# A second fold in a backward row DFT, and its loads spread over the stage before

## The chip, the cores and the metric

The kernel runs on one core of a Trainium2 chip. The metric is the device time of one launch in microseconds; where several runs are shown, it is their median. A core has a matrix engine (TensorE, PE in the profile, with its weight loads shown apart as PEld), three elementwise engines (VectorE or DVE, ScalarE or ACT, GpSimd or POOL), and a queue from which all of this kernel's transfers are issued (SyncE or SP). Matrix products land in PSUM and are copied out by ScalarE or VectorE, which is called an evacuation here.

## The reference

The program computes a two-part block and all of its gradients. With x of 2048 x 448 values in bf16:

- part A: `h = x + irfft2(rfft2(layernorm(x)) * (w_r + 1j*w_i))`, a two-dimensional Fourier filter over rows (448) and columns (2048);
- part B: `out = h + mlp(layernorm(layernorm(h)))`, where the MLP mixes along the 2048 axis: `u = gelu(h^T w1 + b1)`, `y = u w2 + b2`, with 1792 hidden units;
- then the gradients of x, w_r, w_i, w1, b1, w2 and b2 for a given gradient of the output.

The backward pass runs through the MLP first. Its last product gives the gradient of h, called dh. The Fourier filter's backward pass then takes a row DFT of dh, a column DFT, a multiplication with the conjugate filter, and the inverse of both. A DFT is done here as matrix products with tables of cosines and sines. A row of 448 real values has 225 frequencies, kept as 226 columns.

## The kernel before, in words

The 2048 rows are 16 tiles of 128. One Python function writes the whole program; the order of TensorE, VectorE, ScalarE and SP instructions is that of the code. Only GpSimd's instructions are placed by a scheduler. A helper `evac` sends each evacuation to ScalarE or VectorE by a running account of both loads. `defer` puts a transfer some time later in the order of issue.

**The dh stage** is the loop `for t in range(NT)` near line 1183. For tile t, 14 matmuls of 448 columns multiply a transposed tile of w1 (`wT`, four of them in a ring, loaded by a transposing DMA `load_w1T` four tiles ahead) with `du`, the gradient at the hidden layer. The product is normalized back: `ln_a` (one ScalarE operation that leaves PSUM, one small GpSimd operation and one VectorE reduction) and `ln_b` (three VectorE operations), which leaves the tile in `dh`.

**The row DFT** follows inside the same loop, three tiles behind (`LAG`). A row of 448 values is folded first, since cosines are even and sines odd about the middle: `fold_prep`, once for two tiles, writes the sum and the difference of the row's first half and its reversed second half (two VectorE operations of 448 elements). The fold lies in a ring `fold_ring`, three places in the backward pass. `row_a` then takes four pieces of a tile's fold as weights, with a permuting DFT over short groups of rows as the moving side: four matmuls of 128 columns. Its evacuated result is the weights of `row_b`, which does the DFT along the row: for cosine and sine each (index w), two matmuls of 226 columns are summed in PSUM, one for each half of the folded 224 values (index b). Their contraction is 112 deep. The table is `csF`, with a place for each w and b. After every second `row_b`, a transfer regroups the result into `D2`, which the column DFT reads. The regrouping is called the reshuffle here.

**After the loop**, the last rows are done (`for t in range(NT - LAG, NT + 2)`), with matmuls of a weight gradient between them. These come from a list `pending` of generators, from which `fill(n)` takes n steps; they feed on pieces transposed by DMA (`st_load`, of the GELU output in `rE` first) and write weight gradients to memory from `rO` and `rG`. Before the column DFT starts, 40 steps are taken. The column DFT and the filter are in `s2_stage`.

**The loads around it.** The filter W, stored in memory as `w_d` in the forward pass, is read back into `rC` by one load of 1.8 MB after the loop; `rC` holds the output gradient tiles (`go_pt`) until then, the last of which is read by `ln_b` of tile 15. The second weight gradient needs `du` transposed: `load_du`, four transposing transfers of 14 blocks of 128 x 128, issued in `s2_stage` after column groups 3, 7, 11 and 15, into the space of `D2` as that becomes free.

`m448` is a ring of eight 448-element buffers in `r448`; `ln_a` takes two of them for a tile.

Of the kernel before, what the change touches and what calls it, by code (L numbers as in the profile page):

```python
# [13 lines left out]
ALU = mybir.AluOpType  # L14
# [3 lines left out]
P = 128  # L18
S = 2048
D = 448  # L20
DF = 225
KW = 226
F = 1792
NFB = 14
NT = 16
NG = 16
KC = 113
DC = 112
# [11 lines left out]
N_FILL_B = (16, 16, 40, 8, 24, 8)  # L40
INV_SD = 1.0 / float(S * D)
# [78 lines left out]
def kernel(  # L120
# [20 lines left out]
    nc = tc.nc  # L141
# [3 lines left out]
    ve = Meter(nc.vector, load, 1)  # L145
# [68 lines left out]
    def mm(out, lhsT, rhs, start, stop):  # L214
        nc.tensor.matmul(out, lhsT=lhsT, rhs=rhs, start=start, stop=stop)  # L215
        clock[0] += int(np.prod(rhs.shape[1:])) / 2400.0
        run_due()
# [19 lines left out]
    r448 = region("r448", 8 * D)  # L237
# [5 lines left out]
    csF = mem.tile([P, 2, 2, KW], BF16, name="csF")  # L243
# [38 lines left out]
    w_d = dram.tile([P, NG * 2 * KW], BF16, name="w_d")  # L282
# [346 lines left out]
    def fold_prep(src, t2):  # L629
        ft = fold_ring.next()  # L630
        s0 = 2 * t2
        fv = ft[:, 0:2 * D].rearrange("p (s w j) -> p s w j", s=2, w=2)
        a = src[:, s0:s0 + 2, 0:D // 2]
        r = src[:, s0:s0 + 2, D - 1:D // 2 - 1:-1]
        ve.tensor_tensor(out=fv[:, :, 0, :], in0=a, in1=r, op=ALU.add)
        ve.tensor_tensor(out=fv[:, :, 1, :], in0=a, in1=r, op=ALU.subtract)
        folds[t2] = ft

    def row_a(t, R):
        pa = ps_ff()  # L640
        ft = folds[t // 2]
        for k in range(4):
            o = DC * (4 * (t % 2) + k)
            mm(pa[:, k * P:(k + 1) * P], lhsT=ft[:, o:o + P], rhs=R, start=True, stop=True)
        if t % 2 == 0:
            blks[t // 2] = blk_ring.next()
        evac(out=blks[t // 2][:, :, t % 2, :], in_=pa[:].rearrange("p (a b) -> p a b", a=8))

    def row_b(h):
        u, c = divmod(h, 2)  # L650
        if u < 0 or u >= NT // 2:
            return
        pd = ps_ff()
        pv = pd[:, 0:452].rearrange("p (c k) -> p c k", c=2)
        for w in (1, 0):
            for b in range(2):
                mm(pv[:, 1 - w, :], lhsT=blks[u][0:DC, 2 * (2 * w + b) + c].rearrange('p j x -> p (j x)'), rhs=csF[0:DC, w, b, :],
                   start=(b == 0), stop=(b == 1))
        if c == 0:
            css[u] = cs_ring.next()  # L660
        cs = css[u]
        evac(out=cs[:, c], in_=pv)
        if c:
            defer(RESH_LAG, lambda: nc.sync.dma_start(out=D2[u:u + 121:8].rearrange("p g c k -> p (g c k)"),
                                                      in_=cs.rearrange("p x c k -> p (x c k)")), cs)

    def s2_stage(get_x, on_mult, ml, n_fill, gap, make_inv, after_fwd=None, scale=None):
        flush()
        nh = NG // 2
        xs, ys = {}, {}  # L670

        lag = 2 + ml
        for c2 in range(nh + lag):
            if c2 < nh:
                xs[c2] = get_x(c2)
                if make_inv and c2 < 4:
                    gen_inv_s(4 + c2)
                    if c2 in (1, 2):
                        gen_inv_d(c2 - 1)
            for i in range(2):  # L680
                if make_inv and c2 >= 3:
                    next(wp, None)
                    next(wp, None)
                if c2 < nh:
                    g = 2 * c2 + i
                    px = ps_ff()
                    pv = px[:, 0:452].rearrange("p (c k) -> p c k", c=2)
                    mm(pv, lhsT=Vt[:, g, :], rhs=D2[:, g, :, :], start=True, stop=False)
                    mm(pv[:, 0, :], lhsT=Ut[:, g, :], rhs=D2[:, g, 1, :], start=False, stop=False)
                    mm(pv[:, 1, :], lhsT=Un[g], rhs=D2[:, g, 0, :], start=False, stop=True)  # L690
                    evac(out=xs[c2][:, i, :, :], in_=pv, scale=scale)
                if c2 >= lag:
                    s2_inv(2 * (c2 - lag) + i, ys[c2 - lag][:, i, :, :])
                if after_fwd is not None and c2 < nh and g % 4 == 3:
                    after_fwd(g // 4)
                fill(n_fill)
            if ml <= c2 < nh + ml:
                ys[c2 - ml] = on_mult(c2 - ml, xs[c2 - ml])
        if make_inv:
            sc.activation(out=warm, in_=eps_h, func=ACT.Sqrt)  # L700
        fill(gap)
# [56 lines left out]
    pending = []  # L758
# [105 lines left out]
    for c in range(2):  # L864
        sc.copy(out=Rp.rearrange("p (a q b c) -> p c a q b", c=2, q=8, a=4)[:, c],
                in_=Rm[:, 64 * c:64 * c + 64].rearrange("p (q a b) -> p a q b", q=8, a=4))
# [259 lines left out]
                         op0=ALU.mult)  # L1126
    gp_.memset(csF[:, 0, :, 0:1], 0.5)
    ve.tensor_scalar(out=csF[:, :, :, 224:225], in0=csF[:, :, :, 224:225], scalar1=0.5, scalar2=None, op0=ALU.mult)


    dh = cut(rA, 0, NT, D)
    lcol = mem.tile([P, 2 * NT, 3], F32, name="lcol")
# [21 lines left out]
        gen_neg(cut(r2, (2 * NG * KW + 8 * i * P), 8, P), Ut[:, 8 * i:8 * i + 8, :])  # L1154
    Un[:] = [r2[:, 2 * NG * KW + g * P:2 * NG * KW + (g + 1) * P] for g in range(NG)]
    LAG = 3
    st_ring = Ring(ring(rst, 0, 2, 7, P).views + [cut(rS, 6336, 7, P)])
    fold_ring.views.pop()
    order = [(rE, j) for j in range(NFB // 2)] + [(rB, t) for t in range(NT // 2)]
# [2 lines left out]
    def st_load():  # L1162
        if order:
            reg, j = order.pop(0)
            st = st_ring.next()
            nc.sync.dma_start_transpose(out=st, in_=reg[:, j * 1024 + 64:j * 1024 + 960])
            ahead.append(st)


    def rows(t):  # L1170
        if t < NT:
            row_a(t, Rm[:])
        fill(2)
        row_b(t - 2)
        fill(2)

    for t in range(NT):
        wT = w1Ts.pop(0)
        pdh = ps_mm()
        for j in range(NFB):  # L1180
            mm(pdh[:, 0:D], lhsT=wT[:, j, :], rhs=du[:, j, :], start=(j == 0), stop=(j == NFB - 1))
        if t + 4 < NT:
            load_w1T(t + 4)
        pb, tmp, m1, m2, _ = ln_a(t, pdh[:, 0:D], rstd_h[:, t:t + 1], hln[:, t, :], (1.0 + LN_EPS) / D)
        ln_b(pb, tmp, m1, m2, hln[:, t, :], go_pt[:, t, :], dh[:, t, :])
        if t % 2:
            fold_prep(dh, t // 2)
        if t >= NT - 2:
            st_load()
        if t >= LAG:  # L1190
            rows(t - LAG)


    du_t = cut(r2, 0, NFB, 4, P)

    def load_du(q):
        nc.sync.dma_start_transpose(out=du_t.rearrange("p j b q -> p (j b) q")[:, 14 * q:14 * q + 14, :],
                                    in_=rD[:, 14 * P * q:14 * P * (q + 1)])
    def bwd_x(c2):
        return X_ring.next()  # L1200

# [14 lines left out]
    def gw_gen(n, rhs, width, store, ost):  # L1216
        for u in range(n // 2):
# [19 lines left out]
            for c in range(0, 4, 2):  # L1237
# [20 lines left out]

    pending.append(gw_gen(NFB, lambda c, k, a, b: goT[a:b, k, c * 512:(c + 1) * 512], S,
                          lambda j, a, n, o: nc.sync.dma_start(out=out_6[j * P:(j + 1) * P, a:a + n], in_=o[:, 0:n]), ost))  # L1260
    pending.append(gw_gen(NT, lambda c, k, a, b: du_t[a:b, 4 * c:min(NFB, 4 * c + 4), k, :], F,
                          lambda t, a, n, o: nc.sync.dma_start(out=o4[:, t, a:a + n], in_=o[:, 0:n]),
                          Ring(ring(rG, 0, 8, S // 2).views + ost.views)))
    nc.sync.dma_start(out=rC[:, 0:NG * 2 * KW], in_=w_d[:])
    for t in range(NT - LAG, NT + 2):
        if t == NT - 2:
            fill(8)
# [2 lines left out]
        gen_neg(UTn[:, 8 * i:8 * i + 8, :], UTt[:, 8 * i:8 * i + 8, :])  # L1270
    fill(N_FILL_B[2])
    Meter.slack = 4.0
    s2_stage(bwd_x, bwd_mult, 0, N_FILL_B[3], N_FILL_B[4], False, load_du, 2.0 * INV_SD)
    Meter.slack = 2.0
    g_out = w_io(W_view_B, out_2, out_3, True)
    xall = cut(rX, 0, NT, D)
# [68 lines left out]
```

## Time and profile before

| what | us |
|---|---|
| median of 6 runs (369.07 to 372.67) | 370.8 |
| the profiled execution, its own time | 368.74 |
| its span, first to last instruction | 367.0 |
| TensorE busy | 349.6 (95%) |
| VectorE busy | 256.6 (70%) |
| ScalarE busy | 204.1 (56%) |
| GpSimd busy | 72.0 (20%) |

By stage, from windows of the profiled execution: from 200 to 240 us (the dh stage with its row DFT) TensorE is busy all the time, VectorE 7.29, 6.17, 7.03 and 6.34 us of each 10, ScalarE 4.63 to 5.12; the transfers keep the DMA engines busy for a share of 0.88, 0.94, 0.86 and 0.38. From 250 to 260 that share is 1.15.

How to read it: times are microseconds from the span's start, or nanoseconds where marked. A busy TensorE isn't TensorE at its peak, since matmuls are pipelined and each one's record covers its latency, so records overlap; the spacing of starts tells the price of one. A row of a timeline is start, duration, engine, line, operation, what is written and read with shapes, count, and in brackets the idle time before it and what ended it. A row of waits is engine and line, what was waited for, total, times, longest. A row of the chain is start, duration, engine, tile. In a row of windows, each engine's busy time is followed by its instructions in brackets; the last three numbers are TensorE's granted clock, the DMA share and GB/s. L215 is the helper through which all matmuls go, and L79 that of the ScalarE and VectorE operations.

### The profile page before, as it was taken

The numbers are of one execution on the slowest core, as the hardware profiler recorded it, in microseconds if no ns is written. First come the engines' busy times: TensorE is split into PE (matmuls) and PEld (weight loads), VectorE is DVE, ScalarE is ACT, GpSimd is POOL, SyncE is SP. The second block draws the span as 40 slices with busy tenths as digits, with TensorE's granted clock in tenths as the row PEclk, the third lists the DMA queues.
The fourth block names the chain that finished last, engine by engine and source line by source line (L and its number), as shares of the span: only waits on it lengthen the run. The fifth ranks groups of instructions, "written<-read, shape, count | busy, mean of one in ns | idle before, by whom it ended". The sixth has DMA issues, their size and how long they took to land.

```text
span 367.0 us, 6392 instructions
## 1 busy us (share of the span) xinstructions
PE 349.6 (95%) x2133; PEld 186.9 (51%) x2133; DVE 256.6 (70%) x659; ACT 204.1 (56%) x427; POOL 72.0 (20%) x226
## 2 busy tenths in 40 slices
PE   5898997899999999999999999999999999999993
PEld 2355764555645555555555566553454544555541
DVE  5898838982875888593237767664787884689882
ACT  3558746866977453513303444463577674676661
POOL 8567000000220000010002211200000000476750
PEclk9699999999999999999999999999999999999998
DMA  8999999647999999996879799279879889899997
GB/s 203 276 201 239 189 203 170 147 142 259 298 289 353 315 326 234 222 273 177 186 167 176 153 195 182 55 226 290 230 224 225 232 208 263 231 224 269 200 206 242
DMA packets 148393, 81.63 MB, mean 222 GB/s; under 512 B 95560, under 2 KB 140872, under 8 KB 147976
## 3 DMA queue, kind: packets, MB, share of 16 engines
q1 hardware_dynamic: 148360, 81.23, 91.8%
q8 instruction: 16, 0.26, 0.3%
q14 instruction: 17, 0.14, 0.1%
HBM read 27.56 MB, written 23.89 MB: 140 GB/s over the span
## 4 chain that ended last, share of the span: by engine, by line
PE 82%; ACT 5%; DMA 4%; DVE 3%; issue 2%; POOL 2%; SPq 1%; ACTq 0%
PE ps_mm L215 66%; PE ps_ff L215 16%; DMA rO<-in_B_w_dram 2%; ACT rO L79 2%; DMA rA<-in_A_x_dram 1%; ACT rG L79 1%; DVE stats L79 1%; ACT Ut L79 1%; SPq L294 1%; DVE rA L79 1%; DVE r L79 0%; ACT rX L79 0%; POOL nt_f L383 0%; ACT rAT L79 0%; POOL nt_f L384 0%
## 5 line engine op out<-in xcount | busy, mean ns | idle before, releaser
L215 PEld LDWEIGHTS <-r 128*128 128x128 bf16 (+1 forms) x628 | 60.3, 105 | 48.4 <-issue 1.0
L215 PEld LDWEIGHTS <-rS 128*128 128x128 bf16 (+2 forms) x528 | 44.3, 98 | 41.0 <-issue 8.5
L1143 POOL TENSOR_SCALAR lcol<-lcol 128x1 f32<-128x1 f32 x32 | 19.0, 595 | 147.5 <-ACT r L79 147.4
L215 PE MATMUL ps_mm<-rD,r 128*128 128x448 bf16 x224 | 44.5, 352 | 0.0
L215 PE MATMUL ps_mm<-rC,rE 128*128 128x448 bf16 x144 | 36.4, 371 | 3.9 <-DMA rC<-in_grad_out_dram 3.4
L215 PEld LDWEIGHTS <-rst 128*128 128x128 bf16 (+1 forms) x320 | 24.0, 97 | 29.0 <-issue 13.2
L79 ACT CAST rO<-ps_mm 128x512 bf16<-128x512 f32 (+1 forms) x52 | 28.5, 582 | 14.9 <-PE ps_mm L215 14.2
L215 PE MATMUL ps_mm<-rG,rst 128*128 128x512 bf16 (+1 forms) x160 | 35.0, 380 | 0.0
L79 ACT CAST r<-ps_ff 128x452 bf16<-128x452 f32 x54 | 28.9, 538 | 10.0 <-PE ps_ff L215 9.2
L215 PE MATMUL ps_mm<-rB,r 128*128 128x448 bf16 x160 | 31.2, 352 | 0.1
L215 PE MATMUL ps_mm<-r,rst 128*128 128x512 bf16 (+3 forms) x160 | 31.2, 353 | 0.0
L79 ACT ACTIVATE r<-ps_mm,rstd_h 128x448 bf16<-128x448 f32 x16 | 10.1, 634 | 29.3 <-PE ps_mm L215 29.3
L79 DVE CAST rO<-ps_mm 128x512 bf16<-128x512 f32 (+1 forms) x28 | 18.1, 658 | 11.8 <-PE ps_mm L215 11.8
L215 PE MATMUL ps_ff<-csI,rAT 113*128 113x448 bf16 x108 | 24.9, 353 | 0.6 <-ACT rAT L79 0.4
L79 DVE SCALAR_TENSOR_TENSOR r<-ps_mm,b2col,r 128x448 bf16<-128x448 f32 x16 | 10.9, 682 | 19.9 <-PE ps_mm L215 18.4
L79 ACT ACTIVATE r<-rC 128x448 bf16<-128x448 bf16 x16 | 9.1, 571 | 26.7 <-DMA out_dram<-r 20.3
L215 PEld LDWEIGHTS <-rO 128*128 128x128 bf16 (+1 forms) x165 | 15.6, 98 | 12.8 <-DMA rO<-in_B_w_dram 2.5
L79 ACT ACTIVATE rG<-rG 128x896 bf16<-128x896 bf16 x14 | 13.3, 950 | 14.9 <-DVE rG L79 14.7
L215 PE MATMUL ps_mm<-rE,rS 128*128 128x448 bf16 x112 | 21.5, 352 | 0.0
L215 PE MATMUL ps_mm<-rC,rO 128*128 128x448 bf16 x80 | 19.1, 352 | 2.1 <-DMA rO<-in_B_w_dram 2.1
L215 PEld LDWEIGHTS <-rE 128*128 128x128 bf16 x148 | 14.3, 101 | 12.3 <-issue 5.1
L215 PE MATMUL ps_ff<-csF,rS 112*128 112x226 bf16 x128 | 17.7, 260 | 1.7 <-ACT rS L79 1.7
(188 smaller groups left out, 631.2 us busy)
## 6 DMA issues: line engine op xcount, KB each, us to landing
out_dram<-rO SPq DMA_DIRECT2D x34, 256.0 KB
r<-in_B_w_dram SPq DMA_DIRECT2D x5, 1024.0 KB
r<-r SPq DMA_DIRECT2D x16, 226.0 KB
r<-r SPq DMA_DIRECT2D x32, 113.0 KB
rS<-in_B_w_dram SPq DMA_DIRECT2D x4, 896.0 KB
out_dram<-r SPq DMA_DIRECT2D x32, 112.0 KB
out_dram<-rG SPq DMA_DIRECT2D x10, 256.0 KB
rO<-in_B_w_dram SPq DMA_DIRECT2D x2, 1024.0 KB
```

The costliest lines, as they stand in the source:

```text
L79: fn(**kw)
L215: nc.tensor.matmul(out, lhsT=lhsT, rhs=rhs, start=start, stop=stop)
L294: nc.sync.dma_start_transpose(out=wT, in_=B_w2[j * P:(j + 1) * P, :].rearrange("f (t c) -> f t c", c=P))
L1143: gp_.tensor_scalar(out=m1, in0=ms, scalar1=-1.0 / D, scalar2=None, op0=ALU.mult)
```

## The change

Both halves of the folded row are used once more. About the middle of the folded 224 values, the even-numbered frequencies are even and the odd-numbered ones odd (or the reverse for sines). So the fold is folded again into four quarters of 112: `fold_quarters` writes sum and difference of the row's halves into two `m448` places, then sum and difference of those with their reversed halves into the fold. For each w, the two matmuls of `row_b` no longer sum: one makes the 113 even frequencies, the other the 113 odd ones. They need a table with even and odd columns apart (`csB`), made by two copies into the part of `csF` for b = 1, whose old values the backward pass no longer needs. The evacuation puts the columns back in order.

The filter W is read back in four quarters, after tiles 6, 10 and 14 of the dh stage and after the loop. `du` is transposed in one piece of 8 blocks after tile 3 and three pieces of 16 after column groups 5, 9 and 13. The core of the diff:

```diff
+    csB = csF[:, :, 1, :].rearrange("p w (e k) -> p w e k", e=2)
+
+    def fold_quarters(src, t2):
+        ft = fold_ring.next()
+        s0 = 2 * t2
+        i = m448.i % 8
+        assert i % 2 == 0
+        m448.next(), m448.next()
+        pm = cut(r448, i * D, 2, 2, D // 2)
+        fv = ft[:, 0:2 * D].rearrange("p (s k j) -> p s k j", s=2, k=4)
+        a, b = src[:, s0:s0 + 2, 0:D // 2], src[:, s0:s0 + 2, D // 2:D]
+        ve.tensor_tensor(out=pm[:, :, 0, :], in0=a, in1=b, op=ALU.add)
+        ve.tensor_tensor(out=pm[:, :, 1, :], in0=a, in1=b, op=ALU.subtract)
+        lo, hi = pm[:, :, :, 0:DC], pm[:, :, :, 2 * DC - 1:DC - 1:-1]
+        ve.tensor_tensor(out=fv[:, :, 0:4:3, :], in0=lo, in1=hi, op=ALU.add)
+        ve.tensor_tensor(out=fv[:, :, 2:0:-1, :], in0=lo, in1=hi, op=ALU.subtract)
+        folds[t2] = ft
...
-    def row_b(h):
+    def row_b(h, quarters=False):
...
         for w in (1, 0):
             for b in range(2):
+                if quarters:
+                    mm(pq[:, 1 - w, b, :], lhsT=blks[u][0:DC, 2 * (2 * w + b) + c].rearrange('p j x -> p (j x)'),
+                       rhs=csB[0:DC, w, b, 0:KW // 2], start=True, stop=True)
+                    continue
...
-        evac(out=cs[:, c], in_=pv)
+        if quarters:
+            evac(out=cs[:, c].rearrange("p w (j e) -> p w e j", e=2), in_=pq)
+        else:
+            evac(out=cs[:, c], in_=pv)
...
+    for w in range(2):
+        ve.tensor_copy(out=csB[:, w, :, 0:KW // 2], in_=csF[:, w, 0, :].rearrange("p (j e) -> p e j", e=2))
...
+    du_t = [cut(r2, 2048 * q, 4, 4, P) for q in range(3)] + [cut(r2, (2 * KW + P) * NG, 2, 4, P)]
+
+    WQ = (6, 10, 14)
+
+    def load_W(q):
+        a, b = 4 * q * 2 * KW, 4 * (q + 1) * 2 * KW
+        nc.sync.dma_start(out=rC[:, a:b], in_=w_d[:, a:b])
+
+    def load_du(q):
+        n = du_t[q].shape[1] * 512
+        nc.sync.dma_start_transpose(out=du_t[q].rearrange("p j b q -> p (j b) q"), in_=rD[:, 2048 * q:2048 * q + n])
...
-        row_b(t - 2)
+        row_b(t - 2, True)
...
         if t % 2:
-            fold_prep(dh, t // 2)
+            fold_quarters(dh, t // 2)
         if t >= NT - 2:
             st_load()
+        if t == 3:
+            load_du(3)
+        if t in WQ:
+            load_W(WQ.index(t))
         if t >= LAG:
             rows(t - LAG)
...
-    nc.sync.dma_start(out=rC[:, 0:NG * 2 * KW], in_=w_d[:])
+    load_W(3)
...
-    s2_stage(bwd_x, bwd_mult, 0, N_FILL_B[3], N_FILL_B[4], False, load_du, 2.0 * INV_SD)
+    s2_stage(bwd_x, bwd_mult, 0, N_FILL_B[3], N_FILL_B[4], False, {5: lambda: load_du(0), 9: lambda: load_du(1), 13: lambda: load_du(2)}, 2.0 * INV_SD)
```

More of the change, by code (lines that the diff above doesn't have):

```diff
@@ L654, in row_b @@
         pv = pd[:, 0:452].rearrange("p (c k) -> p c k", c=2)
+        pq = pd[:, 0:452].rearrange("p (c e k) -> p c e k", c=2, e=2)
         for w in (1, 0):
             for b in range(2):
+                if quarters:
+                    mm(pq[:, 1 - w, b, :], lhsT=blks[u][0:DC, 2 * (2 * w + b) + c].rearrange('p j x -> p (j x)'),
+                       rhs=csB[0:DC, w, b, 0:KW // 2], start=True, stop=True)
+                    continue
                 mm(pv[:, 1 - w, :], lhsT=blks[u][0:DC, 2 * (2 * w + b) + c].rearrange('p j x -> p (j x)'), rhs=csF[0:DC, w, b, :],
@@ L693, in s2_stage @@
                     s2_inv(2 * (c2 - lag) + i, ys[c2 - lag][:, i, :, :])
-                if after_fwd is not None and c2 < nh and g % 4 == 3:
-                    after_fwd(g // 4)
+                if after_fwd is not None and c2 < nh and g in after_fwd:
+                    after_fwd[g]()
                 fill(n_fill)
@@ L1186 @@
         if t % 2:
-            fold_prep(dh, t // 2)
+            fold_quarters(dh, t // 2)
         if t >= NT - 2:
             st_load()
+        if t == 3:
+            load_du(3)
+        if t in WQ:
+            load_W(WQ.index(t))
         if t >= LAG:
             rows(t - LAG)
[L1194 to L1198, printed above, removed]
     def bwd_x(c2):
@@ L1260 @@
                           lambda j, a, n, o: nc.sync.dma_start(out=out_6[j * P:(j + 1) * P, a:a + n], in_=o[:, 0:n]), ost))
-    pending.append(gw_gen(NT, lambda c, k, a, b: du_t[a:b, 4 * c:min(NFB, 4 * c + 4), k, :], F,
+    pending.append(gw_gen(NT, lambda c, k, a, b: du_t[c][a:b, :, k, :], F,
                           lambda t, a, n, o: nc.sync.dma_start(out=o4[:, t, a:a + n], in_=o[:, 0:n]),
                           Ring(ring(rG, 0, 8, S // 2).views + ost.views)))
-    nc.sync.dma_start(out=rC[:, 0:NG * 2 * KW], in_=w_d[:])
+    load_W(3)
     for t in range(NT - LAG, NT + 2):
```

## The prediction

> **What bounds the kernel now.** I read the page's busy table and chain first, to see which engine sets the end.
>
> ```profile
> PE 349.6 (95%) x2133; PEld 186.9 (51%) x2133; DVE 256.6 (70%) x659; ACT 204.1 (56%) x427; POOL 72.0 (20%) x226
> PE 82%; ACT 5%; DMA 4%; DVE 3%; issue 2%; POOL 2%; SPq 1%; ACTq 0%
> L215 PE MATMUL ps_ff<-csF,rS 112*128 112x226 bf16 x128 | 17.7, 260 | 1.7 <-ACT rS L79 1.7
> ```
>
> TensorE carries the end. The third row holds the matmuls that the change narrows: 64 of the 128 are the backward ones. Its 260 ns is the latency of one; the price is the spacing, taken below. Next, the waits of the weight loads (PE's own list is empty) from 106 to 361 us, where waits for data would show:
>
> ```profile
> PEld L215 <- issue: 23.6, 60, 0.5
> PEld L215 <- ACT r L79: 0.4, 1, 0.4
> ```
>
> One wait for another engine, 0.4 us, in 255 us. So from the dh stage on, a TensorE nanosecond removed is a nanosecond off the end, unless it turns into a wait. The chain inside the dh stage gives the rhythm:
>
> ```profile
> 222.44 0.62 PE ps_ff L215 x8
> 223.05 2.65 PE ps_mm L215 x14
> 225.70 0.62 PE ps_ff L215 x8
> ```
>
> and the timeline of TensorE splits the 0.62:
>
> ```profile
> 205.94 0.39 PE L215 MATMUL ps_ff<-Rm,rS 128*128 128x128 bf16 x4
> 206.16 0.56 PE L215 MATMUL ps_ff<-csF,rS 112*128 112x226 bf16 x4
> 206.56 2.81 PE L215 MATMUL ps_mm<-rD,r 128*128 128x448 bf16 x14
> ```
>
> Start to start: four 128-column matmuls take 0.22 us (55 ns each), four 226-column ones 0.40 (99 ns), fourteen 448-column ones 2.65 (189 ns). The period is 3.27 us.
>
> Last, the place after the loop where TensorE first needs the last fold (tiles 14 and 15): timelines of VectorE and of the weight loads.
>
> ```profile
> 239.56 0.62 DVE L79 CUSTOM_DVE_ANT_0 r<-r,rB 128x448 bf16<-128x448 bf16 x1 [1.27 <-ACT r L79]
> ...
> 241.16 0.39 DVE L79 TENSOR_TENSOR rA<-r,rC 128x448 bf16<-128x448 bf16 x1
> 241.66 0.69 DVE L79 TENSOR_TENSOR rS<-rA 128x448 bf16<-128x448 bf16 x2
> 242.27 1.28 DVE L79 CAST rO<-ps_mm 128x512 bf16<-128x512 f32 x2
> ```
> ```profile
> 242.43 0.42 PEld L215 LDWEIGHTS <-rS 128*128 128x128 bf16 x4
> ```
>
> The fold ends at 242.35 and its first weight load starts at 242.43. No time is lost, but the slack is under 0.1 us. Everything earlier in the loop has more.
>
> **What the Trainium skill says.** "TensorE: Matmul & The Clock Gate", section "Back-to-back issue gap", prices a warm matmul of N columns at N/2.4 + 2.5 ns: 189, 97 and 56 for 448, 226 and 128, against 189, 99 and 55 here. For 113 it gives 49.6 (an estimate; no such matmul runs here). The same section's 81 ns for a sustained stream at N = 128 isn't seen: row_a's have new weights each and stand 55 apart. "VectorE: DVE Perf Modes", section "Side-by-side: where the cycles go for N=2048 bf16", gives about 150 fixed cycles and two bf16 elements per cycle at 0.96 GHz for a packed two-input operation: (150 + 224)/0.96 = 390 ns for 448 elements; the trace has 388 to 392, with the reversed operand of the old fold too. One-element mode would be 623 ns.
>
> **The change part by part.** The sum is made on the profiled execution (span 367.0, its own time 368.74), and the difference is carried to the median of 370.8.
>
> *Narrower matmuls.* 16 calls of row_b with 4 matmuls each; count and weights stay, columns go from 226 to 113. At 49.6 ns: 64 x (99 - 50) = -3.1 us. Bounds: if the reload of weights can't go below the 55 seen at 128 columns, 64 x 44 = -2.8; if the narrower matmul gains nothing, 0, which row_a's 55 speaks against; below 47 (113/2.4) nothing streams, so at best -3.3. I take -3.1.
>
> *Second fold.* Eight pairs of tiles get two more 448-element additions each. The old two took 0.69 together, and a dependent one starts 0.03 after its producer's end (VectorE's timeline), so four end 0.74 later: 8 x 0.74 = 5.9 us of VectorE. In the loop it is covered: a pair of tiles keeps VectorE 2.71 (206.90 to 209.61) plus 1.99 (210.16 to 212.15) = 4.70 us; after, 5.44 in a pair of periods of 2 x (3.27 - 0.20) = 6.14. The fold of an odd tile is needed two tiles later. It ends 0.95 + 1.99 + 0.11 + 1.43 = 4.48 us after that tile's last matmul has gone out, and the next row_a that reads it comes 0.42 + 2.65 + 0.42 + 2.65 = 6.14 after. Slack 1.6, and 1.2 for the first, where row_b doesn't run yet. The two m448 slots that a fold takes leave the ring of 8 long enough: the slot a tile's first ScalarE write gets was last used at least two tiles before.
>
> *The last fold.* This cover is gone after the loop. With T the end of the dh matmuls (238.61), row_a(14) went out at T + 4.04. Before it stand two row_b calls, now 0.39 us shorter: it would go at T + 3.65. The fold was done at T + 3.74, now at T + 4.48; 0.07 for the signal and 0.10 for the weights put row_a(14) at T + 4.65. TensorE is in order, so it stands for 1.0 us and all fills behind it too: +1.0. Late next are three VectorE evacuations queued behind the fold; the psum buffer that they free is needed after two more fills and row_b(12), at T + 5.5, the first being free at T + 5.1. No second stall.
>
> *Evacuations of row_b.* They write bf16 at a stride of two elements. The plain one took 0.55 us of ScalarE; no row shows a strided one. At twice that, ScalarE goes from 1.6 to 2.2 us per period of 3.07. Hidden either way: 0.
>
> *Two copies into csF.* 452 elements of VectorE before the first tile, in its idle time of 1.24 us before 193.27: 0, at most 0.6 if that cover weren't there.
>
> *Loads moved.* W goes from one 1.8 MB load at 241.58 to quarters after tiles 6, 10, 14 and 15; 8 of the 56 du blocks go to tile 3, the other 48 from four transposes to three. On SP's queue the early du piece stands between the w1T loads of tiles 7 and 8, W quarters behind those of tiles 10 and 14; the third and fourth stand right behind the first two st transposes, with a reshuffle into D2 behind each. Sources and targets are long free but for the last quarter, which waits for dh of tile 15 as the whole load did, and holds the same reshuffle behind it. By the trace's semaphore updates w1T landed 223.64, 227.13 and 229.89 for tiles 13 to 15 and was used at 229.59, 232.85 and 236.12: 5.7 to 6.2 us early. The added 1.2 MB before tile 15 must find DMA time. Windows of the old stage (DMA share and GB/s are the last two numbers):
>
> ```profile
> 207.00:208.00 1.00, 1.00 (x7) 0.52 (x6) 0.89 (x3) 0.78 (x2) 0.59 (x1) 1.00 0.24 55
> 209.50:211.00 1.50, 1.50 (x13) 0.94 (x11) 0.84 (x4) 1.50 (x4) 0.64 (x1) 1.00 0.09 19
> 223.00:224.00 1.00, 1.00 (x7) 0.48 (x5) 0.66 (x3) 1.00 (x4) 0.65 (x1) 1.00 0.08 19
> 234.00:238.00 4.00, 4.00 (x27) 2.37 (x26) 3.17 (x10) 1.64 (x4) 0.64 (x1) 1.00 0.00 0
> 242.00:258.00 16.00, 16.00 (x96) 7.41 (x95) 8.79 (x16) 7.01 (x13) 0.00 (x0) 1.00 1.09 280
> ```
>
> There are holes between the loads and a wide one at the end. At the 280 GB/s of the last line 1.2 MB is 4.3 us, most of it into holes: 0. The relief after 241 pays nothing either: the last reshuffle into D2 landed at 255.83 and was first read at 257.61, so TensorE wasn't waiting for it. Its margin grows.
>
> Sum: -3.1 + 1.0 = -2.1: span 364.9, profiled time 366.6, median 368.7.
>
> **The rivals.** *No stall at the last fold* (367.7, the whole 3.1): TensorE would have to arrive later than I reckon. The 0.08 us between fold and weight load speaks against.
>
> *The reload of weights sets the pace* at 55 ns: -2.8 + 1.0, 369.0. The 98 ns of one weight load in the groups speaks for a floor somewhere; the 55 ns stream bounds it.
>
> *VectorE becomes the bound.* The new operations work on runs of 112. In one-element mode for the two of them, 0.23 each: the pair takes 5.9 of 6.14, the tail stall grows to 1.5, 369.2. If all four fell to that mode, 6.4 exceeds 6.14, TensorE drifts by 0.24 in each of six pairs and stands 1.9 at the end: -3.1 + 1.4 + 1.9, 371.0.
>
> *Slower: the w1T transposes arrive late.* Place: the last dh tiles. Price: each us of landing beyond the margin is a us of TensorE. With no holes and the stage's present 175 GB/s, 1.2 MB is 6.8 us by tile 15, against 6.2 less the 1.9 by which TensorE runs ahead: a stall of 2.5, 371.2. It cancels the gain from 2.1 us of stall, and makes the kernel slower by over 0.5% (1.9 us) from 4.0, that is at a net 145 GB/s: 372.7. For it speaks a DMA share of 0.86 to 0.94 from 200 to 230; the holes above speak against.
>
> *The change doesn't do what it says*: column order and operations are as described in the built program, so what is left is only a 113-column matmul that costs as much as a 226-column one: 0 + 0.6 (T + 4.65 against T + 4.04), 371.4.
>
> **How the numbers follow.** Forecast 0.47, no stall 0.12, weight floor 0.16, VectorE slower 0.12, late w1T 0.09, no gain 0.04. Half a per cent, about what a measurement of this kernel can tell from no change, is 1.9 us, so the line lies at 368.9, just above my forecast: I count three quarters of the forecast's chance and all of no stall as faster, some of the weight floor too: 0.52. Slower by over 0.5%: late w1T's worse half and a little for what I don't see, 0.08. The rest, 0.40, is within. The range, 366.9 to 370.6, runs from no stall less 0.8 of spread in the medians (the six runs span 3.6) up to a partial loss in VectorE or DMA; the forecast's own is 368.0 to 369.4.
>
> **What would show it.** Row_b's matmuls 50 ns apart and a period of 3.07; one wait of about 1 us of the weight loads for VectorE before row_a(14), and none in the loop; four fold operations in 1.4 us; w1T transposes landing at least 2 us before use; the same tail after the last matmul. I am wrong if the 113-column matmuls stand at 55 or more, if weight loads wait for a DMA in the loop, or if a new wait shows in the spectral stage.

## The result, and the profile after

The changed kernel takes 367.3 us (median of 27 runs, 366.07 to 369.82). The kernel before, run beside it, takes 370.4 us (median of 62 runs, 367.62 to 373.37). The ratio of runs on the same chip is 0.9929, with a 95% interval from 0.9913 to 0.9945: 2.6 us faster, between 2.0 and 3.2.

The profiled execution of the change is a poor place to see that. Its span is 366.4 us against 367.0, and its own time, 369.82, is the longest of the 27 and even above the 368.74 of before. The stretch from the first matmul product of the MLP to the last matmul shows why. Views by tile and by source line give the landmarks: after the tiles' names and the count come the shortest, median and longest record in ns, then the first and last start. Before:

```profile
L215 PE MATMUL ps_mm<-rB,r x160: 349/352/355, 104.3 to 147.0; 128*128 128x448 bf16 x160
L215 PE MATMUL ps_mm<-r,rS x96: 269/379/389, 305.2 to 361.0; 128*128 128x512 bf16 x54, 64*128 64x512 bf16 x18, 128*128 128x256 bf16 x18, 64*128 64x256 bf16 x6
```

After:

```profile
L215 PE MATMUL ps_mm<-rB,r x160: 349/352/354, 105.6 to 148.3; 128*128 128x448 bf16 x160
L215 PE MATMUL ps_mm<-r,rS x96: 269/379/390, 304.3 to 360.2; 128*128 128x512 bf16 x54, 64*128 64x512 bf16 x18, 128*128 128x256 bf16 x18, 64*128 64x256 bf16 x6
```

From the first start (104.31 and 105.56) to the last start (361.0 and 360.2) it was 256.7 us and is 254.6. The 1.25 us by which this execution started the MLP later lies in work that the change doesn't touch: over the twelve executions profiled here that start falls anywhere from 102.5 to 105.6, with the same order of matmuls ahead of it. In the two latest, this one and that of the loads alone further down, TensorE was granted half its clock for 3.4 us from about 62 us on, and in the others it wasn't; TensorE's 351st matmul comes 0.2 us earlier here than before, and its 371st 1.5 us later. The comparisons below therefore use this stretch, called **the path**, beside the ratio of times. It went from 256.71 to 254.60, that is 2.1 us less.

The busy table and the engines' shares of the chain, from the page of the change:

```profile
PE 347.7 (95%) x2133; PEld 184.0 (50%) x2133; DVE 262.1 (72%) x677; ACT 206.0 (56%) x427; POOL 70.2 (19%) x226
PE 79%; ACT 6%; DMA 5%; DVE 4%; issue 2%; POOL 2%; SPq 1%; ACTq 0%; DVEq 0%
```

VectorE has 18 more instructions and 5.5 us more work (two additions in each of eight folds, two copies), and TensorE, still the bound, has shorter ones. The rhythm of the dh stage, from the chain:

```profile
207.35 0.43 PE ps_ff L215 x8
207.78 2.65 PE ps_mm L215 x14
210.43 0.43 PE ps_ff L215 x8
```

and the same stretch in TensorE's timeline:

```profile
207.18 0.39 PE L215 MATMUL ps_ff<-Rm,rS 128*128 128x128 bf16 x4
207.41 0.37 PE L215 MATMUL ps_ff<-csF,rS 112*128 112x113 bf16 x4
207.62 0.92 PE L215 MATMUL ps_mm<-rD,r 128*128 128x448 bf16 x4
```

The four narrow matmuls go from 207.41 to 207.62; over the stage their starts stand 52 ns apart, where the 226-column ones stood 99 apart. The period is 3.08 us instead of 3.27. Then the waits of the weight loads from 106 to 361 us:

```profile
PEld L215 <- issue: 24.0, 61, 0.5
PEld L215 <- DVE rS L79: 1.2, 1, 1.2
```

There is one wait for VectorE, and it is at the last fold. VectorE's timeline there:

```profile
240.55 0.39 DVE L79 TENSOR_TENSOR rA<-r,rC 128x448 bf16<-128x448 bf16 x1
240.98 0.69 DVE L79 TENSOR_TENSOR r<-rA 128x448 bf16<-128x448 bf16 x2
241.78 0.69 DVE L79 TENSOR_TENSOR rS<-r 128x448 bf16<-128x448 bf16 x2
242.39 1.88 DVE L79 CAST rO<-ps_mm 128x512 bf16<-128x512 f32 x3
```

and the weight loads:

```profile
240.79 0.55 PEld L215 LDWEIGHTS <-rst 128*128 128x128 bf16 x4 [0.42 <-issue]
242.53 0.23 PEld L215 LDWEIGHTS <-rS 128*128 128x128 bf16 x4 [1.19 <-DVE rS L79]
```

The last fold, four operations from 240.98 to 242.47, ends 60 ns before `row_a(14)` loads its first weights. TensorE had been there 1.2 us earlier by its weight loads. By its matmuls, it stood for 0.86: the start of the last one ahead, at 241.45, and that of the next lie 1.08 us apart instead of 0.22. The idle time in brackets is shorter, because a record covers a matmul's latency:

```profile
242.53 0.40 PE L215 MATMUL ps_ff<-Rm,rS 128*128 128x128 bf16 x4 [0.70 <-DVE rS L79]
```

So the account of the path is 64 x (98.8 - 52.2) ns = -3.0, and +0.86: -2.1, which is what the path shows.

The w1T transposes, which the moved loads were put among, landed later but in time: by the trace's semaphore updates, for tiles 11, 13, 14 and 15, at 220.45, 225.01, 227.43 and 232.94, with the first matmul of each at 223.03, 229.19, 232.27 and 235.35. Tiles 11 and 15, whose transposes are the next ones behind a W quarter, have margins of 2.6 and 2.4 us; tile 15 had 6.1 before. (The expectations below have 2.7 and 2.6: they took the times of use from the chain, which lie 0.16 later.) This execution is a tight one: in the second of the same kernel, further down, tile 15's margin is 3.6.

### The profile page after: what moved, and what is told of

Read it like the earlier page. It is cut to its first block, busy times and chain, and to the rows that moved or that the text cites. A ratio compares the mean times of both kernels' runs of the same rounds, so it can differ in the third digit from the quotient of the medians.

```text
span 366.4 us, 6419 instructions
## 1 busy us (share of the span) xinstructions
PE 347.7 (95%) x2133; PEld 184.0 (50%) x2133; DVE 262.1 (72%) x677; ACT 206.0 (56%) x427; POOL 70.2 (19%) x226
## 4 chain that ended last, share of the span: by engine, by line
PE 79%; ACT 6%; DMA 5%; DVE 4%; issue 2%; POOL 2%; SPq 1%; ACTq 0%; DVEq 0%
PE ps_mm L215 64%; PE ps_ff L215 15%; DMA rO<-in_B_w_dram 2%; ACT rO L79 2%; ACT rG L79 1%; DMA r<-r 1%; DMA rA<-in_A_x_dram 1%; DVE stats L79 1%; DVE r L79 1%; ACT Ut L79 1%; SPq L294 1%; DVE rA L79 1%; DVE rS L79 1%; ACT rX L79 0%; ACT r L79 0%
## 5 line engine op out<-in xcount | busy, mean ns | idle before, releaser
L215 PEld LDWEIGHTS <-rS 128*128 128x128 bf16 (+2 forms) x528 | 42.7, 98 | 41.6 <-issue 8.5
L1170 POOL TENSOR_SCALAR lcol<-lcol 128x1 f32<-128x1 f32 x32 | 17.5, 548 | 148.0 <-ACT r L79 147.8
L79 ACT CAST r<-ps_ff 128x452 bf16<-128x452 f32 x53 | 30.5, 577 | 8.7 <-PE ps_ff L215 7.9
L215 PE MATMUL ps_mm<-rC,rO 128*128 128x448 bf16 x80 | 20.1, 367 | 2.3 <-DMA rO<-in_B_w_dram 2.3
L79 ACT CAST rS<-ps_ff 128x512 bf16<-128x512 f32 x31 | 18.3, 589 | 4.2 <-PE ps_ff L215 4.0
```

Source lines behind the costliest of these rows:

```text
L79: fn(**kw)
L1170: gp_.tensor_scalar(out=m1, in0=ms, scalar1=-1.0 / D, scalar2=None, op0=ALU.mult)
```

## The experiments

The working theory is that of the forecast, called A in the expectations: narrow matmuls give their columns, the last fold takes one microsecond back, the loads are worth nothing. Each rival is named in its expectation.

### The loads alone

```diff
-        row_b(t - 2, True)
+        row_b(t - 2)
...
-            fold_quarters(dh, t // 2)
+            fold_prep(dh, t // 2)
```

The two copies into `csB` go as well; the loads stay where the change put them.

> The changed kernel with its moved loads (W in quarters, du in one early and three later pieces), but with the old single fold, the old table and the 226-column matmuls. Theory A, that the loads were hidden before and still are: the time of the kernel before within its uncertainty, ratio 0.998 to 1.002, TensorE without a new wait. Theory B, that the measured 2.6 us exceed the 2.1 of the fold's account because the loads were worth something: 0.5 us faster, ratio 0.9985 or below, with transfers after the loop landing earlier and something on TensorE's path shorter. If the early loads cost something, a wait of weight loads for a DMA inside the dh loop.

Measured: ratio 0.9981 (0.9961 to 1.0001), 369.35 against 370.17. The waits of the weight loads from 110 to 361 us are those of before:

```profile
PEld L215 <- issue: 22.0, 55, 0.5
PEld L215 <- ACT r L79: 0.4, 1, 0.4
```

and the path, from 105.4 to 362.1 in the landmarks, is 256.70 against 256.71. The ratio fits both theories, since 0.9981 lies in the range of the one and within the bound of the other; the path and the waits speak for A. The moved loads alone bring nothing that the path shows.

### The second fold alone

```diff
-        if t == 3:
-            load_du(3)
-        if t in WQ:
-            load_W(WQ.index(t))
...
-    load_W(3)
+    nc.sync.dma_start(out=rC[:, 0:NG * 2 * KW], in_=w_d[:])
```

`du` is again transposed in four pieces of 14 blocks, after column groups 3, 7, 11 and 15.

> The changed kernel with its second fold and narrow matmuls, but W in one load after the loop and du in four pieces of 14 blocks after column groups 3, 7, 11 and 15, as before. Theory A: 2.1 us faster than the kernel before (64 matmuls cheaper by 46 ns, one stand of 0.9 us), ratio 0.9943, not to be told from the full change. Theory B: the whole W load now delays the last reshuffle into D2 past its first use, since TensorE gets there sooner: a wait of weight loads for a DMA at the start of the column DFT and a smaller gain, ratio 0.996 or above.

Measured: ratio 0.9927 (0.99 to 0.9955), 367.49 against 370.17; path 254.81. The gain is there without the loads, but for 0.2 us of the path. So is the stall, from 200 to 250 us:

```profile
PEld L215 <- issue: 2.5, 6, 0.4
PEld L215 <- DVE rS L79: 1.2, 1, 1.2
```

### The fold kept, the matmuls wide

```diff
-        row_b(t - 2, True)
+        row_b(t - 2)
```

The four-part fold is made, but the backward row DFT reads its quarters as if they were halves, so its result is not the DFT. VectorE has the work of the second fold, and TensorE keeps its wide matmuls. This is the cost of the edit without its gain.

> The changed kernel with the second fold, the table copies and the moved loads, but the 226-column matmuls of before (so the backward row DFT takes quarters for halves, and its result is not the DFT). It has the cost of the change without its gain. Theory A: the fold's 5.9 us of VectorE are hidden in the loop, and TensorE stands only at row_a(14), by 4.53 - 4.04 = 0.5 us: 0.5 us slower than before, ratio 1.0013. Theory B, VectorE limits the loop: several waits for VectorE, 2 us or more slower, ratio 1.005.

Measured: ratio 1.0011 (0.9989 to 1.0033), 369.87 against 370.17. `row_a(14)` came 0.5 us late, and from the first dh matmul to the last matmul it is 171.93 us against 171.42 before: +0.5. (The path as a whole is 1.0 longer; the other half is a wait for a w1 transpose that ended at 128.5 us, in a stage ahead of the change.) From 200 to 250 us the waits are

```profile
PEld L215 <- issue: 2.1, 5, 0.4
PEld L215 <- DVE rS L79: 0.8, 1, 0.8
```

The same place waits less than in the change, since TensorE comes there later by two wide `row_b`. This is the forecast's own subtraction at the last fold with one term taken out. In the loop the second fold costs nothing: no wait appears there.

### More fills ahead of the last fold

If TensorE stands because it comes too early, five steps of the weight gradient, taken from after the loop to before it, should fill the time.

```diff
-            fill(8)
+            fill(13)
...
-    fill(N_FILL_B[2])
+    fill(N_FILL_B[2] - 5)
```

> The changed kernel with 13 instead of 8 fill steps ahead of row_a(14), and 35 instead of 40 ahead of the column DFT. Five steps are five matmuls of 512 columns, 1.08 us, more than the 0.86 us for which TensorE stands there. Theory A: the wait for VectorE is gone and nothing takes its place: 0.9 us faster than the change, ratio to the kernel before 0.9905 to 0.991 if the change measures 0.993. Theory B: the later evacuations queue behind the fold on VectorE, so the fills wait for a psum buffer in its place: no faster than the change, with a wait of TensorE for an evacuation.

Measured: ratio 0.9928 (0.9904 to 0.9952), 367.51 against 370.17, the same as the change. The stall did go. The weight loads of `row_a(14)`, with no wait in brackets:

```profile
241.39 0.42 PEld L215 LDWEIGHTS <-rS 128*128 128x128 bf16 x4
```

From the last dh matmul to the spectral stage it is 18.23 us instead of 18.95. But from there to the last matmul it is 104.79 instead of 103.41, and the path, 255.27, is longer than the change's. With the order of the steps the running account in `evac` had given other evacuations to VectorE. TensorE's timeline shows the largest consequence:

```profile
353.28 1.78 PE L215 MATMUL ps_mm<-r,rS 128*128 128x512 bf16 x8
355.70 1.99 PE L215 MATMUL ps_mm<-r,rS 64*128 64x512 bf16 x8 [0.64 <-DVE rO L79]
```

A weight-gradient product waits for an evacuation: VectorE first runs three operations of the gradient of x (354.06 to 355.31), and the evacuation of 256 columns follows them at 355.23. Of two smaller steps of TensorE, behind the matmuls at 241.77 and 336.22 (0.16 and 0.27), the chain puts the second to an evacuation by VectorE too, and tells no cause for the first. The stall was removed and more than its 0.86 us given back, most of it 95 to 115 us later; the rival was right in kind, though the place was not one that it named.

### The last fold split by tile

Tile 14's fold needs only tile 14. If it is done when `dh` of tile 14 is ready, only tile 15's half is left for the end.

```diff
-        if t % 2:
+        if t >= NT - 2:
+            fold_one(dh, t)
+        elif t % 2:
             fold_quarters(dh, t // 2)
```

`fold_one` has the same four operations on 224 elements, into the tile's half of its own place in the fold ring, and `row_a` reads that place for these two tiles.

> The changed kernel in which tiles 14 and 15 are folded each by itself, tile 14 while tile 15 is still multiplied (eight VectorE operations of 224 elements in place of four of 448); the order of fills and the share of evacuations between ScalarE and VectorE stay as they are. Theory A: the wait at row_a(14) is gone, since its fold is done about 3 us earlier, and row_a(15) comes about 1.3 us after row_a(14), by when its own fold is done: 0.9 us faster than the change, from the start of the MLP's first product to the last matmul 253.7 us in place of 254.6, ratio to before 0.9905 to 0.991. Theory B, as with the fills moved: a wait for an evacuation later takes the 0.9 us back.

Measured: ratio 0.9897 (0.9861 to 0.9934), 364.35 against 368.28; path 253.74, which is 0.86 less than the change's and just the time for which TensorE stood there. From 110 to 361 us the weight loads wait for no other engine. The list is

```profile
PEld L215 <- issue: 23.2, 58, 0.5
```

VectorE's timeline shows tile 14's fold, and that of the weight loads `row_a(14)` without a wait, 2.85 us earlier than in the change's trace:

```profile
236.47 0.46 DVE L79 TENSOR_TENSOR r<-rA 128x224 bf16<-128x224 bf16 x2
237.03 0.46 DVE L79 TENSOR_TENSOR rS<-r 128x224 bf16<-128x224 bf16 x2
```
```profile
239.68 0.42 PEld L215 LDWEIGHTS <-rS 128*128 128x128 bf16 x4
```

(1.8 us of the 2.85 are the earlier start of the MLP in this execution.) This is the best version that computes all of the outputs. Its interval by time still overlaps that of the change, so the path and the missing wait, of one execution, are what sets them apart.

### More loads behind the w1T transposes

How near was the slower rival? Each W quarter after tiles 6 and 10 is followed by one more 463 KB load on the same queue (three more in the second kernel), from `w_d` into `rO`, whose contents nobody reads then.

```diff
         if t in WQ:
             load_W(WQ.index(t))
+            for i in range(1 if t < 14 else 0):
+                nc.sync.dma_start(out=rO[:, 1808 * i:1808 * (i + 1)], in_=w_d[:, 1808 * i:1808 * (i + 1)])
```

> The changed kernel with one more load of a W quarter (463 KB, to a place that nobody reads) behind each of the quarters after tiles 6 and 10. In the change the w1T transposes of tiles 11 and 15 land 2.7 and 2.6 us before their first matmul. Theory A: at 280 to 400 GB/s one more load puts them 1.2 to 1.7 us later, no wait, and the dh loop keeps its 47.0 us. Theory B, the loop's transfers are already at the limit: a wait of weight loads for in_B_w_dram.

> The same with three more loads behind each of the two quarters (2.8 MB in all). Theory A: 3.5 to 5 us later at tiles 11 and 15, so waits of 1 to 2.3 us at the first and up to as much at the second, the dh loop 48 to 51 us, the whole 1 to 4 us slower than the change. If the loop stays at 47.0 us, the margin was of no account and the DMA engines had far more room than the shares say.

Measured with one more load: 366.9 in a single run beside 368.28, which is too little to compare times; path 255.87, which is 1.3 longer than the change's. In TensorE's timeline a dh product, that of tile 15, waits for its transpose:

```profile
233.12 0.37 PE L215 MATMUL ps_ff<-csF,rS 112*128 112x113 bf16 x4
234.59 2.82 PE L215 MATMUL ps_mm<-rD,r 128*128 128x448 bf16 x14 [1.10 <-DMA r<-in_B_w_dram]
```

That is the sign of theory B, which the margin in the change had not led me to expect. The transpose was issued at 225.76 and landed at 234.54. In the change it was issued at 225.89, on an MLP start 2.0 us later, and SP's timeline shows what it met:

```profile
224.57 0.58 SPq L1190 DMA_DIRECT2D rC<-w_d  x1
225.25 0.54 SPq L690 DMA_DIRECT2D r<-r  x1
225.89 4.33 SPq L1035 DMA_TRANSPOSE r<-in_B_w_dram  x1
```

Behind one W quarter the issue of the transpose holds SP for 4.33 us, where it took 1.48 before, and from issue to landing it takes 7.05 us instead of 4.16. With a second load ahead it takes 8.8. So the extra load delays the transpose twice: against the MLP's start it is issued 1.9 us later, and it takes 1.7 us longer to land. My estimate had counted one of the two.

The sizes vary, though. Over the seven executions with one quarter ahead, the issue of this transpose holds SP for 2.7 to 4.3 us and it lands after 5.8 to 7.05; over the three with none ahead these are 1.5 to 1.6 and 4.1 to 4.2. And with the second load fifteen of the sixteen updates of its semaphore were in by 233.14, 0.2 us before TensorE was ready for these weights; only the last came at 234.54. That the extra load uses up the margin is thus seen in one execution, and hangs there on one late update.

Measured with three more: ratio 1.0108 (1.0066 to 1.015), 372.64 against 368.28; path 262.11, that is 7.5 longer than the change's, where theory A had 1 to 4 us. The waits for the transposes (4.9 us in two, from 110 to 361) are

```profile
PEld L215 <- DMA r<-in_B_w_dram: 4.9, 2, 4.2
```

and three windows, whose last three numbers are TensorE's granted clock, the DMA share and GB/s:

```profile
233.70:237.90 4.20, 0.17 (x4) 0.00 (x1) 2.59 (x8) 1.54 (x4) 0.46 (x1) 0.86 0.97 147
237.90:243.00 5.10, 5.05 (x14) 2.10 (x15) 0.00 (x0) 0.00 (x0) 0.00 (x0) 0.50 0.97 226
243.00:247.00 4.00, 4.00 (x31) 1.98 (x29) 2.54 (x8) 3.26 (x7) 0.64 (x1) 0.93 0.00 0
```

In the longer wait, 4.2 us, TensorE's granted clock falls to half. By the shares in the first and the third window that lasts from about 236.7 us, while TensorE still waits, to about 243.6. The next 14 matmuls stand 373 ns apart instead of 189, and the 4 of `row_a` behind them 107 instead of 56: 2.8 us more. "TensorE: Matmul & The Clock Gate" of the Trainium skill, section "What's actually happening", tells of this: after at least one idle window of about 3.4 us the clock falls to half, and it comes back after at least one busy window of that length. The trace agrees on the fall, and here the clock came back after 5.6 us of matmuls. Not all traces here agree on the idle time: the half clock near 62 us in the change's execution came 3.3 us after the start of a gap in TensorE's records of only 2.3 us, and gaps of 2.0 to 2.2 us at the same place were followed by it in one other execution (2.05) and not in three (2.04, 2.15, 2.24). So the 7.5 us are 4.9 of waits and 2.8 of clock, less 0.2 by which the stall at the last fold is shorter (0.70).

The slower rival was a real mechanism. The change is free of it by 2.4 us of landing time at tile 15 in one execution and 3.6 in the other; three more loads of 463 KB after each of two tiles use up more than that, and one more did in the single execution taken.

### Fewer columns still

The narrow matmul takes 64 columns instead of 113, and its evacuation copies 64. The rest of the frequencies of the backward DFT are left out, so part of the gradients is not computed.

```diff
-                    mm(pq[:, 1 - w, b, :], ...
+                    mm(pq[:, 1 - w, b, 0:64], ...
-                       rhs=csB[0:DC, w, b, 0:KW // 2], ...
+                       rhs=csB[0:DC, w, b, 0:64], ...
```

> The changed kernel with only the first 64 of each 113 columns in row_b (the other frequencies of the backward row DFT are left out; the evacuation copies what was made). Theory A: the spacing goes on following the columns, 64/2.4 + 5 = 32 ns in place of 52, 64 matmuls save 1.3 us, and row_a(14) stands 0.15 us longer: 1.1 us faster than the change. Theory B: the reload of weights sets a floor near 50 ns, spacing and time unchanged.

Measured: ratio 0.9888 (0.9843 to 0.9933), 364.21 against 368.28; path 253.45, which is 1.15 less than the change's. The starts stand 30.5 ns apart, as theory A has it. The chain shows the period at 3.00:

```profile
204.57 0.35 PE ps_ff L215 x8
204.92 2.65 PE ps_mm L215 x14
```

There is no floor from reloading the weights at 55 ns or at 52. Of the further 64 x 21.7 ns = 1.4 us, 0.2 went into the stall at the last fold, which grew from 0.86 to 1.04.

### The split fold with the old loads

The loads were worth nothing alone. Is that still so, once TensorE no longer stands at the last fold? This kernel is the split fold with the loads of the kernel before.

> The second fold with tiles 14 and 15 folded apart, and all loads where they were before (W in one load after the loop, du in four pieces). Theory A, the moved loads earn nothing: 253.7 us from the start of the MLP's first product to the last matmul, as with the moved loads, ratio to before 0.991, the w1T transposes landing as early as before. Theory B, they are needed once TensorE no longer stands: the last reshuffle into D2 (2.3 us early in the run with the fold alone) comes too late and the column DFT waits for a DMA; ratio 0.993 or above.

Measured: ratio 0.9931 (0.9906 to 0.9957), 365.87 against 367.96; path 254.76, which is 1.0 longer than with the moved loads. The weight loads from 200 to 260 us no longer wait for VectorE, but for a DMA:

```profile
PEld L215 <- issue: 5.3, 13, 0.4
PEld L215 <- DMA rS<-rE: 1.0, 1, 1.0
```

The chain tells which:

```profile
241.72 0.54 SPq L704
242.31 8.40 DMA rS<-rE
250.76 2.98 PE ps_mm L215 x14
```

It is a transpose of the GELU output for the fills, 8.4 us on its way. The whole W load of 1.8 MB was issued 4.1 us before it, with two reshuffles and two writes of results in between, and landed at 247.43 by its semaphore, so it was under way for most of that time. In the split fold with the moved loads the same transpose takes 3.2 us and lands 4.5 us before its first use. TensorE stands 0.71 us for it. The other 0.3 of the 1.0 I have not followed to a place. So theory B was right that the loads are needed, but not in the place: the late transfer is this one and not the last reshuffle. In the kernel with the second fold alone the transpose takes 6.6 us and lands 1.1 us before its use. The stall of 0.86 there gives it most of that margin; why the transpose takes 1.8 us longer still in the split fold stays open.

### The change once more

The change again, beside the kernel above and the same kernel before.

> The changed kernel itself, beside the one above on the same chip: ratio to before 0.993 if the first measurement holds, 0.9943 if only what TensorE's path shows is left; 254.6 us from the start of the MLP's first product to the last matmul.

Measured: ratio 0.9928 (0.9902 to 0.9954), 365.69 against 367.96; path 254.61. The weight loads wait as in the first run:

```profile
PEld L215 <- issue: 23.2, 58, 0.5
PEld L215 <- DVE rS L79: 1.2, 1, 1.2
```

### All together

| kernel | path us | TensorE stands after the loop | ratio |
|---|---|---|---|
| before | 256.71 | no | 1 |
| loads alone | 256.70 | no | 0.9981 |
| second fold, old loads | 254.81 | 0.86 for VectorE | 0.9927 |
| the change, twice | 254.60, 254.61 | 0.86 both times, for VectorE | 0.9929, 0.9928 |
| split fold, old loads | 254.76 | 0.71 for a transpose | 0.9931 |
| split fold, moved loads | 253.74 | no | 0.9897 |

The two parts of the remedy don't add up one by one. With the old loads, the split fold brings 0.05 us; with the old fold order, the moved loads bring 0.2; both together bring 1.1. The fills are late for two reasons of about the same size, and taking one away leaves the other. That rests on the paths and waits, one execution each but for the change, whose two agree to 0.01 us; by time the intervals of the last two rows overlap (0.9906 to 0.9957 and 0.9861 to 0.9934).

## Why the prediction was right

The forecast was 368.7 against a median of 370.8: -2.1. Measured is 367.3, or -2.6 by the ratio, with -2.0 at the interval's end. The time is inside the range (366.9 to 370.6) and on the side that had most of the chance. Of the 1.4 us between forecast and time, 0.4 is that the median of before came down from 370.8 to 370.4 with more runs, 0.5 that the two medians differ by more (3.1) than the ratio of runs on the same chips gives (2.6), and 0.5 that the ratio gives more than the forecast; this last is taken up below. The time alone doesn't prove the forecast: 367.3 lies below the forecast's own 368.0 to 369.4 and nearer to the 367.7 of the rival without a stall, whose -3.1 the interval (-2.0 to -3.2) holds too. What decides between the two is the trace, which has the stall, and the path.

*Narrower matmuls.* Forecast -3.1 at 50 ns; measured -3.0 at 52. The estimate from the Trainium skill's N/2.4 + 2.5 (section "Back-to-back issue gap", as in the prediction) was 2.6 ns low. The mechanism held, and the 64-column run shows that it goes on below 113.

*Second fold in the loop.* Forecast hidden; it is: four operations in 1.49 us against 1.43, no wait in any of the loop's tiles, and with wide matmuls only the last fold's stall shows.

*The last fold.* Forecast +1.0, with `row_a(14)` at T + 4.65 (T being the end of the dh matmuls); measured 0.86, at T + 4.53. T was 238.00, the fold ended at T + 4.47 (forecast 4.48), and the weights followed after 0.06 instead of the 0.17 allowed for signal and load: that is the 0.1 too much. That VectorE's three late evacuations make no second stall held as well: from the last dh matmul to the spectral stage the change lost nothing beyond the 0.86. That this stall was real time on the path, and not slack, the split fold shows: 0.86 came back.

*Strided evacuations.* Bounded between 0.55 and 1.1 us of ScalarE. The group in the dh stage, by form, has

```profile
L79 ACT CAST r<-ps_ff 128x452 bf16<-128x452 f32 x15 | 10.3, 685 | 0.5 <-PE ps_ff L215 0.5
```

685 ns against 547 for the plain one: hidden, as forecast. The copies into `csB` took 0.28 us each in VectorE's idle time: 0.

*Loads moved.* Forecast 0, and alone they are. The step behind it was only half right. No TensorE wait arose, so the time holds, and the wide hole did fill: in the page's slice from 229 to 238 us the rate goes from 55 to 154 GB/s. But I had priced the loads as bandwidth, at 4.3 us of it, and not what they do to the transfer behind them: the transpose behind the second quarter held SP for 2.9 us longer and took 2.9 us longer to land, and tile 15's margin fell from 6.1 to 2.4 (in the second execution 1.3, 1.7 and 3.6). The forecast's "at least 2 us before use" was met with 0.4 to spare in the first. And "the relief after 241 pays nothing" holds for the change only, where the stall at the last fold comes first; without that stall the moved loads are worth 1.0. I had looked at the last reshuffle alone (5.6 us early now, 1.8 before) and not at the transposes for the fills.

*The rivals.* No stall: the stall is in both traces of the change. Weight floor: the 52 and 30.5 ns rule it out. VectorE as the bound: its reversed runs of 112 take 388 ns for 448 elements as the old ones did, and nothing drifted:

```profile
L79 DVE TENSOR_TENSOR rS<-r 128x448 bf16<-128x448 bf16 x16 | 5.5, 388 | 0.6
```

Late w1T: not in the change, and shown with more loads. No gain: the interval and the 52 ns rule it out.

**What stays open.** The path gives -2.1, the ratio -2.6. The interval's end, -2.0, holds the path's figure, but the ratio came out as 0.9929 and 0.9928 twice. The tail after the last matmul (5.96 us before, 6.28 and 5.58 in the two executions of the change, 5.6 to 7.1 over all kernels here) and the head before the MLP vary by more than this from one execution to the next, so one profile of each can't tell whether half a microsecond lies there. The change is hardly the reason: for all nine other measurements with an interval the time by the ratio is likewise 0.5 to 1.4 us lower, against before, than the path has it, and for the loads alone, whose path is that of before, it is 0.7. What they share is the one profiled execution of the kernel before, with 368.74 us one of its faster ones. That it stands for the others is not shown, and no run here settles it.

## What to carry to other kernels

When a change shortens the bound engine and lengthens another, look for the last repetition: in a loop the longer chain hides behind the next tile, and after the loop nothing is behind it, so one end effect (here 0.86 of 3.0 us) is most of the loss, and doing the last item in smaller pieces gets it back. Before you call a part of a change worthless, take the neighbouring stall away first: the moved loads brought next to nothing (0.2 us of the path) until the fold's stall was gone, and 1.0 us then. Judge a load put on a queue by what is issued behind it as well as by its bytes.

## What the runs showed of the hardware

- Matmuls with weights 112 deep and new weights each time stand 98.8, 52.2 and 30.5 ns apart at 226, 113 and 64 columns: about N/2.4 + 4 to 5 ns. Those with 128-deep weights stand 189.2 and 55.9 apart at 448 and 128 columns, which is N/2.4 + 2.5, the formula of the Trainium skill's "TensorE: Matmul & The Clock Gate", section "Back-to-back issue gap". No floor from the reload of weights was met.
- An evacuation of 128x452 values from float32 to bf16 at a stride of two elements took ScalarE 685 ns, and 547 packed.
- The w1T transpose of tile 15 took 4.1 to 4.2 us from issue to landing in three executions without a W quarter ahead of it, 5.8 to 7.05 in seven with one of 463 KB (and a reshuffle) ahead, and 8.8 in the one with two loads ahead; its issue held the queue for 1.5 to 1.6 us without and 2.7 to 4.3 behind the one load, and so delayed what was behind it.
- In a wait of 4.2 us TensorE's granted clock fell to half about 3 us after the last matmul had gone out, and stayed there for the first 5.6 us of matmuls after the wait: 448 columns took 373 ns instead of 189. In two executions a half clock of 3.4 us also followed gaps of only 2.05 and 2.3 us, and in three it did not follow gaps of 2.04 to 2.24.
